# Sink attention and mixer: two heads share each transpose, and value products run on crossed 64x64 quarters

## The chip, the cores and the metric

The kernel runs on one core of one Trainium2 chip. The metric is the device time of one execution in microseconds (us), a median over runs. Five engines work side by side: PE (matrix products; PEld loads its weights), DVE (VectorE), ACT (ScalarE), POOL (GpSimd) and SP, which here only issues DMAs. PE writes to PSUM, which has eight banks; DVE and ACT read PSUM, POOL works on SBUF alone.

## The reference, cut to what matters

```python
# q, k, v: [4, 8, 768, 64]; n_sink = 4, window = 128
scores = scale * np.matmul(q, k.transpose(0, 1, 3, 2))
keep = is_sink | ((rel >= 0) & (rel < window))     # rel = query - key
a = softmax(np.where(keep, scores, -1e9))
x = np.matmul(a, v)                                # heads side by side: [4, 768, 512]
h = x.transpose(0, 2, 1) @ U @ V                   # U: 768 x 32, V: 32 x 768
u = x + h.transpose(0, 2, 1)
out = u + np.maximum(u @ w_ch1, 0.0) @ w_ch2       # 512 -> 2048 -> 512
```

Everything is float32. The two large products of the feed-forward part are made as sums of products of high and low parts, which is most of PE's work.

## The kernel before

**Stages.** Batch 0 comes first and alone: attention, then the rank-32 mixing (`mix_start`, `mix_half`, `mix_end`), about 62 us in which PE has no feed-forward work yet, since that needs batch 0's mixed activations. From there PE runs the feed-forward part of batch 0 (`ffn`, lines 1111 to 1133) and then of batches 1 to 3 (`ffn_joint`, line 1281), and the attention of batches 1 to 3 is laid between these products. DVE, ACT and POOL meanwhile also rebuild the weights from raw 64-bit words (lines 151 to 159: `nr`, `nt`, then a joining sum into `big` or `spare`), split them into high and low parts (line 656 or 657, and line 663 or 665 for the difference) and evict PE's banks.

**One unit of attention** is a pair of heads times one half of the queries; a half takes 64 of each 128 queries, six slices of 64. There are 4 batches x 4 pairs x 2 halves = 32 units. `scores` (line 794) multiplies on 64x64 quarters of the PE array: the two heads are the row halves, two slices the column halves. A slice sees 192 keys; the oldest 64 and the newest 64 of them share 64 columns, since a query row sees a key of just one of the two. A copy under a mask folds them (line 802). Line 807 adds the mask and takes the minimum of a 128x132 block (4 sinks, 64 folded keys, 64 full keys), line 810 is the exponential, lines 817 to 831 normalise, lines 836 to 838 set the sink columns aside.

**Transposes** (line 849): each head's three blocks of 128 queries x 128 keys go through PE into a bank, one bank for each head. The result `oph` holds for each slice the probabilities against its own key block and against the block before it. So the bank is copied whole (128x384, line 656 on ACT or 657 on DVE), the part for the block before is made with a triangular mask (128x320, line 855 on DVE from the bank or line 857 on POOL from the copy), and POOL then masks the copy in place (128x384, line 860). That is three operations a head, six a unit.

**Values** (line 891): for one unit alone (batch 0), twelve products of 128 rows by 64 columns, the two heads on the two column halves. In batches 1 to 3 both halves of a pair are joined (`JOINED`): 22 products on 64x64 quarters, for the folded keys, and 22 on 128x64 halves. Each product of float32 appears as two rows of the trace. One copy a half brings the result into `xT`.

**Order.** `Plan` simulates the engines with a duration for each step, places every step on one of the engines that its `any` allows, and fixes the order of each engine; `MOVES` and `SEED` are a list of pseudo-random changes to the priorities that set the order. Rings of buffers (`NOP` of `oph`, eight banks) limit how far it runs ahead.

Of the kernel before, what the change touches and what calls it, by code (L numbers as in the profile page):

```python
# [9 lines left out]
F32 = mybir.dt.float32  # L10
# [11 lines left out]
P = 128  # L22
# [11 lines left out]
TW = SW + G  # L34
# [25 lines left out]
SEED = 30000000  # L60
# [14 lines left out]
JOINED = True  # L75
# [15 lines left out]
NOP = 4  # L91
# [93 lines left out]
class Masks:  # L185


    def __init__(self, nc, pool, room):
        self.nc, self.work = nc, pool
        self.m = pool.tile([P, 4, SW], F32, name="mask")  # L190
# [4 lines left out]
        nc.gpsimd.iota(raw, [[-G, 2], [-1, G]], base=P, channel_multiplier=1)  # L195
# [4 lines left out]
        nc.gpsimd.memset(self.m[lo, 0, G:P], -NEG)  # L200
        v.tensor_copy(t[lo, 0:2], raw[lo])
        v.tensor_scalar(t[hi, 0:2], raw[hi], -float(G), None, ALU.add)
        v.tensor_scalar(self.now, t[:, 1], float(G), None, ALU.is_ge)
        v.tensor_scalar(self.past, t[:, 1], float(G), None, ALU.is_lt)
        v.scalar_tensor_tensor(t[:, 0], self.now, -float(P), t[:, 0], ALU.mult, ALU.add)
        v.scalar_tensor_tensor(t[lo, 2], self.past[lo], FAR, t[lo, 0], ALU.mult, ALU.add)
# [3 lines left out]
    def fill(self, ns, w):  # L210
        nc, m, t, lo, hi = self.nc, self.m, self.t, self.lo, self.hi
        v, copy = nc.vector, nc.scalar.copy
        ck = self.work.tile([P, 3, NS], F32, name="m_ck")
        v.tensor_scalar(ck[:, 2], self.cix[:, 0], ns, None, ALU.is_lt)
        v.scalar_tensor_tensor(ck[:, 0:2], self.s, w, ck[:, 2].unsqueeze(1).broadcast_to([P, 2, NS]), ALU.is_ge, ALU.mult)
        rows = lambda x: x.rearrange("p a b -> p (a b)")
        for part, at, src in ((slice(0, P), (1, slice(0, P)), rows(t[:, 0:2])), (hi, (0, slice(0, P)), rows(t[hi, 0:2])),
                              (lo, (0, slice(0, G)), t[lo, 2])):
            v.tensor_scalar(m[part, at[0], at[1]], src, w[part], -NEG, ALU.is_ge, ALU.mult)
# [364 lines left out]
class Fast:  # L584
# [191 lines left out]
    def scores(self, half, js, t0, q, kr, row):  # L776
# [4 lines left out]
        def pieces(kb):  # L781

            if kb:
                return (((0, (kb - 1) * SW + NS + half * G, TW),))
# [1019 lines left out]
```

## Time and profile before

| | us |
|---|---|
| median of 3 runs (670.09 to 672.14) | 670.67 |
| the profiled execution | 671.74 |
| its span, first to last instruction | 670.0 |
| PE busy | 648.8 (97%) |
| DVE / ACT / POOL busy | 527.9 / 426.6 / 248.6 |

A busy PE is not a PE at its peak, because consecutive matrix products overlap; so what PE's share says is that there are few gaps. Which of the other engines matters is read stage by stage: a table of windows gives the busy time of each engine in a stretch, the chain of waits says which engine's instructions followed one another up to the end of a stretch, and the groups by line give a duration for each kind of instruction.

### The profile page before, as it was taken

What the parts mean: (1) busy time and instruction counts of PE and PEld (TensorE: products, weight loads), DVE (VectorE), ACT (ScalarE), POOL (GpSimd) and SP (SyncE); (2) the same over time, 40 slices, a digit from 0 to 9 for tenths busy, and PEclk for the clock granted to TensorE, in tenths of its full rate; (3) what the DMA queues carried; (4) which work ended last, traced back from release to release, by engine and by line L of the source; (5) the groups of instructions that cost most, each with busy time, mean ns of one, the idle gap of its engine ahead of it and who ended that gap; (6) DMA issues with size and microseconds to landing.
All of it is one profiled execution on the core that took longest, in us unless ns stands there. A gap on an engine that the chain in (4) does not pass through costs nothing.

```text
span 670.0 us, 15532 instructions
## 1 busy us (share of the span) xinstructions
PE 648.8 (97%) x5302; PEld 599.0 (89%) x5302; DVE 527.9 (79%) x1481; ACT 426.6 (64%) x1186; POOL 248.6 (37%) x320
## 2 busy tenths in 40 slices
PE   7898999999999999999999999999999999999996
PEld 6665888888889889999989899999999999999996
DVE  6999999889999888688887699578537964773483
ACT  6986788998674379875696774455347626534551
POOL 4741533556435244556365644011212401120120
PEclk8999999999999999999999999999999999999999
DMA  8569999999799799997899778979877789878782
GB/s 272 194 215 349 335 385 321 344 291 353 250 327 359 249 310 384 368 302 239 294 299 361 262 220 260 313 212 326 250 242 254 255 299 365 265 236 265 248 270 95
DMA packets 111720, 191.57 MB, mean 286 GB/s; under 512 B 10256, under 2 KB 46608, under 8 KB 111632
## 3 DMA queue, kind: packets, MB, share of 16 engines
q1 hardware_dynamic: 111200, 189.90, 85.0%
q8 instruction: 44, 0.72, 0.4%
q10 hardware_dynamic: 432, 0.59, 0.3%
q14 instruction: 44, 0.36, 0.2%
HBM read 141.17 MB, written 49.28 MB: 284 GB/s over the span
## 4 chain that ended last, share of the span: by engine, by line
PE 78%; DVE 14%; DMA 4%; issue 1%; ACT 1%; POOL 1%; POOLq 0%; SPq 0%; DVEq 0%; ACTq 0%
PE bank L1281 51%; PE bank L1133 7%; PE bank L891 4%; PE bank L794 4%; PE bank L849 2%; PE bank L1111 2%; PE bank L1113 2%; PE bank L1112 2%; DMA w<-ws 2%; DVE nt L157 1%; DVE p L807 1%; DVE spare L158 1%; DVE w L663 1%; DVE nr L154 1%; DVE spare L663 1%
## 5 line engine op out<-in xcount | busy, mean ns | idle before, releaser
L1281 PE MATMUL bank<-w,w 128*128 128x384 f32 x792 | 156.6, 339 | 1.3 <-DMA w<-ws 1.3
L1281 PEld LDWEIGHTS bank<-w,w 128*128 128x128 f32 x792 | 138.3, 188 | 3.9 <-issue 1.8
L810 ACT ACTIVATE p<-p,mn 128x132 f32<-128x132 f32 x192 | 75.6, 397 | 11.8 <-DVE mn L807 11.3
L1281 PE MATMUL bank<-w,spare 128*128 128x384 f32 x348 | 68.0, 338 | 0.0
L1286 DVE TENSOR_TENSOR big<-bank,big 128x384 f32<-128x384 f32 x84 | 45.0, 552 | 24.8 <-PE bank L1281 24.2
L1281 PEld LDWEIGHTS bank<-w,spare 128*128 128x128 f32 x348 | 61.6, 188 | 0.3 <-DVE w L663 0.2
L1133 PE MATMUL bank<-w,hh 128*128 128x512 f32 x192 | 61.3, 400 | 0.0
L807 DVE CUSTOM_DVE_ANT_0 p<-bank,mask 128x132 f32<-128x132 f32 x192 | 47.7, 289 | 0.1
L665 POOL TENSOR_TENSOR w<-uh,w 128x384 fp32r<-128x384 f32 x18 | 19.9, 1106 | 74.2 <-ACT w L656 63.5
L1111 PE MATMUL bank<-ul,w 128*128 128x384 f32 x128 | 44.5, 347 | 0.7 <-POOL ul L665 0.6
L656 ACT CAST w<-ul 128x384 fp32r<-128x384 f32 x57 | 29.1, 513 | 24.7 <-PE bank L1281 21.5
L857 POOL TENSOR_SCALAR_AFFINE_SELECT oph<-oph 128x320 f32<-128x320 f32 x48 | 28.4, 606 | 43.3 <-ACT oph L656 42.8
L1113 PE MATMUL bank<-uh,w 128*128 128x384 f32 x128 | 43.1, 337 | 0.0
L1112 PE MATMUL bank<-uh,w 128*128 128x384 f32 x128 | 43.1, 336 | 0.0
L1281 PE MATMUL bank<-spare,w 128*128 128x384 f32 x210 | 42.1, 339 | 0.0
L665 POOL TENSOR_TENSOR spare<-spare 128x128 f32<-128x128 f32 (+1 forms) x43 | 29.8, 706 | 32.6 <-DMA ws<-spare 11.4
L794 PE MATMUL bank<-kp,qp 64*64 64x196 f32 (+3 forms) x840 | 39.9, 324 | 1.4 <-DMA kp<-in_k_dram 1.4
L1133 PEld LDWEIGHTS bank<-w,hh 128*128 128x128 f32 x192 | 34.8, 188 | 6.4 <-issue 2.0
L663 DVE TENSOR_TENSOR spare<-spare 128x128 f32<-128x128 f32 (+1 forms) x97 | 38.1, 418 | 1.9 <-ACT spare L656 1.3
L1133 PE MATMUL bank<-w,hl 128*128 128x512 f32 x96 | 38.1, 397 | 1.1 <-DVE hl L1122 1.1
L831 POOL TENSOR_TENSOR p<-p,r 128x396 f32<-128x396 f32 x30 | 26.5, 890 | 31.1 <-DVE r L820 26.3
L891 PEld LDWEIGHTS bank<-oph,vp 128*64 128x64 f32 (+1 forms) x1200 | 33.7, 136 | 4.6 <-issue 2.0
(281 smaller groups left out, 1645.8 us busy)
## 6 DMA issues: line engine op xcount, KB each, us to landing
w<-ws SPq DMA_DIRECT2D x132, 256.0 KB, 4.3
w<-wd SPq DMA_DIRECT2D x102, 256.0 KB, 4.2
big<-in_w_dram SPq DMA_DIRECT2D x32, 512.0 KB, 6.3
ws<-spare SPq DMA_DIRECT2D x32, 512.0 KB, 5.6
spare<-ws SPq DMA_DIRECT2D x60, 256.0 KB, 4.1
wd<-w SPq DMA_DIRECT2D x32, 384.0 KB, 6.2
spare<-wd SPq DMA_DIRECT2D x42, 256.0 KB, 3.7
vp<-in_v_dram SPq DMA_DIRECT2D x15, 384.0 KB, 5.1
```

The costliest lines, as they stand in the source:

```text
L663: ways = {"DVE": (dve(n), lambda: nc.vector.tensor_tensor(dst(), a(), b(), op), pool)}
L665: ways["POOL"] = (gps(n), lambda: nc.gpsimd.tensor_tensor(dst(), a(), b(), op), True)
L794: nc.tensor.matmul(st()[a * G:(a + 1) * G, x * TW + to:x * TW + to + wd], qr()[at, q0:q0 + G], kr()[at, k0:k0 + wd], start=True, stop=True ...
L807: add("DVE", dve(SW), lambda st=st, x=x, j=j, part=part, at=at: nc.vector.tensor_tensor_reduce(part(), st()[:, x * TW + half * G:x * TW + ...
L810: add("ACT", act(SW) + 0.22, lambda part=part, at=at: nc.scalar.activation(part(), part(), AF.Exp, bias=at(mn), scale=-1.0, accum_out=at(sm)),
L891: nc.tensor.matmul(pa()[i * D:(i + 1) * D, c:c + (hi - lo) * G], vr()[at, i, kb, :], mv, start=pa not in begun, stop=last, skip_group_chec ...
L1111: nc.tensor.matmul(ph()[:, :CH], wh, ul()[:, c, :], start=n == 0, stop=False)
L1112: nc.tensor.matmul(ph()[:, :CH], wl, uh()[:, c, :], start=False, stop=False)
L1113: nc.tensor.matmul(ph()[:, :CH], wh, uh()[:, c, :], start=False, stop=n == NC - 1)
L1133: nc.tensor.matmul(acc[k](), a()[:, sl], w()[:, :, at, m:m + P].rearrange("p d o j -> p o d j"), start=not begin and i == 0 and j == 0, st ...
L1281: nc.tensor.matmul(bank()[:, :CH], w()[:, at:at + P], u()[:, d, :] if n > 1 else u(), start=first and i == 1, stop=last and i == 3 * n, sk ...
L1286: add("DVE", dve(CH), lambda: nc.vector.tensor_tensor(x(), bank()[:, :CH], t(), ALU.add), r=(bank,) if t is x else (bank, t), w=(x,), prio ...
```

## The change

**Order of the columns.** For the first head of a pair the key tile gives 2 sinks and then 64 keys for each block, for the second head 64 keys and then 2 sinks (`BW` = 66 columns a block; the layout of `k` in memory changes with it). The reduction writes its result interleaved: column 2c of a 132-wide block belongs to one 66-column block, column 2c + 1 to the other, a step of two floats. The two heads of a query block now lie side by side in `p`. So in the 264 columns of both heads every second one, from a suitable start, is a folded key of the first head (64 of them) and then of the second head (64).

**Transposes.** One bank takes both heads' folded keys, another both heads' full keys: still six transposes of 128x128 a unit, read with a step of two floats. Only the folded bank needs masks: DVE writes both of them straight from the bank (128x384 and 128x320, new line 862). The full bank is copied once into a new tile `opf`. POOL's masking steps are gone.

**Values.** First and second head of a unit now lie on partitions 0 to 63 and 64 to 127, so all value products are 64x64. Two units are always joined (two halves of a pair; in batch 0, two pairs of the same half). The first unit's heads go to column halves 0 and 1, the second unit's to 1 and 0, "crossed", so that four products fill four different quarters; the two heads of a unit are different row halves of the array and write to the same bank, on different partitions. 24 products are for folded keys (20 of them 128 columns wide), 20 to 24 for full keys (64 wide). Because the second unit's heads come out swapped, its result is copied in two pieces of 64 partitions.

**Order.** `SEED` and `MOVES` are another list, so the whole order changes in detail.

```diff
-TW = SW + G
+BW = G + 2
+TW = 3 * BW
...
-SEED = 30000000
+SEED = 510000000
...
-JOINED = True
+VALUES = 2.1
...
-NOP = 4
+NOP = 3
+NOF = 2
...
             for x, j in enumerate(js):
-                part = lambda p=p, i=i, j=j: p()[:, i, j]
+                part = lambda p=p, i=i, j=j: p()[:, j, i]
...
-                    part(), st()[:, x * TW + half * G:x * TW + half * G + SW], self.mask[:, 2 * half + min(j, 1)],
+                    part().rearrange("p (c x) -> p x c", x=2), split(st()[:, at0:at0 + SW]),
+                    split(self.mask[:, 2 * half + min(j, 1), 2 * i:2 * i + SW]),
...
-    def transposes(self, i, half, t0, p):
+    def transposes(self, half, t0, p):
...
-                nc.tensor.transpose(tr()[:, u * P:(u + 1) * P], p()[:, i, u, c:c + P], self.ident)
-        add("PE", 0.30, mms, r=parts + [res], w=(tr,), prio=t0)
-        v3 = lambda: tr()[:, :CH].rearrange("p (u j) -> p u j", u=NB)
-        top, prev = lambda: res()[:, :, 1, :], lambda: res()[:, 1:, 0, :]
-        self.copy(CH, top, v3, psum=True, r=(tr,), w=((res, 1),), prio=t0)
-        self.plan.any({
-            "DVE": (dve(CH - G), lambda: nc.vector.tensor_tensor(
-                prev(), v3()[:, 1:], self.tri[:, half].unsqueeze(1).broadcast_to([P, NB - 1, G]), ALU.mult)),
-            "POOL": (0.126 + (CH - G) * 0.914e-3, lambda: nc.gpsimd.affine_select(
...
-        add("POOL", 0.126 + CH * 0.914e-3, lambda: nc.gpsimd.affine_select(
...
+        for at, box in ((NS + 1 - half, res), (NS + half, full)):
+            tr = self.bank()
...
+                    nc.tensor.transpose(tr()[:, u * P:(u + 1) * P], p().rearrange("p u i w -> p u (i w)")[:, u, at:at + 2 * P - 1:2], self.ident)
...
+        for k, n, to in ((0, NB, lambda: res()[:, :, 1, :]), (1, NB - 1, lambda: res()[:, 1:, 0, :])):
+            add("DVE", dve(n * G), lambda k=k, n=n, to=to: nc.vector.tensor_tensor(
+                to(), v3()[:, NB - n:], self.tri[:, k].unsqueeze(1).broadcast_to([P, n, G]), ALU.mult),
+                r=(banks[0],), w=((res, k),), prio=t0)
+        self.copy(CH, full, lambda: banks[1]()[:, :CH].rearrange("p (u j) -> p u j", u=NB), psum=True,
+                  r=(banks[1],), w=(full,), prio=t0)
...
-    def values(self, parts, t0, vr, xT):
+    def values(self, parts, t0):
...
+        for u in range(NB):
+            for part, (half, *_) in enumerate(parts):
+                wide.append((part, 0, 2 * u + half, u, min(2, NB - u)))
+                if u or half:
+                    slim.append((part, 1, 2 * u + half - 1, u, 1))
+        todo = wide + slim
...
+                    at, to = slice(i * D, (i + 1) * D), (i ^ part) * D
...
+                    nc.tensor.matmul(banks[part]()[to:to + D, u * G:(u + n) * G], vr()[at, block, :], mv,
+                                     start=part not in begun, stop=last, skip_group_check=True)
...
+            for to in (slice(0, P),) if part == 0 else (slice(0, D), slice(D, P)):
+                src = to if part == 0 else slice(D - to.start, D - to.start + D)
+                self.copy(CH, lambda to=to, cols=cols, xT=xT: xT()[to, cols], lambda src=src, part=part: banks[part]()[src, :CH],
+                          psum=True, r=(banks[part],), w=((xT, half),), prio=t0)
...
+            parts.append(self.attend(b, pair, half, t0, q, kr, vr, self.x[b][pair]))
+            if len(parts) == 2:
+                self.values(parts, t0)
+                parts = []
```

**Where the order moves.** Line numbers shift by a few between the two kernels: the fold is line 802 before and 807 after, the reduction 807 and 812, the exponential 810 and 816, DVE's joining sum 158 and 159, POOL's 159 and 160.

DVE in the middle of batch 0's attention, before (`oph` are transposed probabilities, `big` and `nr` raw weights and a scratch tile):

```order
L657 COPY oph_520<-bank_181 128x6x64
L657 COPY pair384a<-psink 128x384
L157 SCALAR_TENSOR_TENSOR nt<-big_101,nr 128x192
L151 TENSOR_SCALAR nr<-big_103 128x384
L820 RECIPROCAL r<-r 128x6
L802 COPY_PREDICATED bank_182<-past,bank_182 128x2x64
L802 COPY_PREDICATED bank_185<-past,bank_185 128x2x64
L807 ISA p_568,mn<-bank_182,mask 128x132
L807 ISA mn 128x1
L855 TENSOR_TENSOR oph_520<-bank_181,tri 128x5x64
```

The same place after:

```order
L158 SCALAR_TENSOR_TENSOR nt<-big_101,nr 128x192
L660 COPY pair384a<-psink 128x384
L152 TENSOR_SCALAR nr<-big_103 128x384
L862 TENSOR_TENSOR oph_551<-bank_182,tri 128x6x64
L862 TENSOR_TENSOR oph_551<-bank_182,tri 128x5x64
L826 RECIPROCAL r<-r 128x6
L807 COPY_PREDICATED bank_183<-now,bank_183 128x2x64
L807 COPY_PREDICATED bank_186<-now,bank_186 128x64
```

Every unit now has two masks of DVE next to each other, where before a unit had a copy or a mask on DVE now and then.

DVE at the end of batch 0's attention, before (`big_103`, `big_104` hold the two halves of V, `vst` its split form):

```order
L154 TENSOR_SCALAR nr<-nr 128x512
L157 SCALAR_TENSOR_TENSOR nt<-big_104,nr 128x384
L155 TENSOR_SCALAR nr<-nr 128x512
L663 TENSOR_TENSOR vst_785<-big_103,vst_785 32x384
L158 TENSOR_TENSOR big_104<-nt,big_104 128x384
L855 TENSOR_TENSOR oph_798<-bank_182,tri 128x5x64
L855 TENSOR_TENSOR oph_801<-bank_184,tri 128x5x64
L663 TENSOR_TENSOR vst_785<-big_104,vst_785 32x384
```

and after:

```order
L158 SCALAR_TENSOR_TENSOR nt<-big_104,nr 128x384
L156 TENSOR_SCALAR nr<-nr 128x512
L862 TENSOR_TENSOR oph_848<-bank_183,tri 128x6x64
L862 TENSOR_TENSOR oph_848<-bank_183,tri 128x5x64
L158 SCALAR_TENSOR_TENSOR nt<-big_105,nr 128x512
L666 TENSOR_TENSOR xhl_865<-bank_182,xhl_865 64x384
L1037 TENSOR_SCALAR pst_918<-bank_185 128x128
L666 TENSOR_TENSOR vst_795<-big_104,vst_795 32x384
```

The joining sums of V (`big<-nt,big`) have left DVE.

POOL over the same stretch, before:

```order
L159 TENSOR_TENSOR big_101<-nt,big_101 128x192
L836 COPY psink<-p_568 128x2x3x4
L857 AFFINE_SELECT oph_763<-oph_763 128x5x64
L831 TENSOR_TENSOR p_665<-p_665,r 128x396
L860 AFFINE_SELECT oph_763<-oph_763 128x6x64
L860 AFFINE_SELECT oph_776<-oph_776 128x6x64
L860 AFFINE_SELECT oph_801<-oph_801 128x6x64
L860 AFFINE_SELECT oph_798<-oph_798 128x6x64
L159 TENSOR_TENSOR spare_189<-nt,spare_189 128x512
```

and after:

```order
L160 TENSOR_TENSOR big_103<-nt,big_103 128x384
L837 TENSOR_TENSOR p_616<-p_616,r 128x3x132
L842 COPY psink<-p_616 128x3x8
L837 TENSOR_TENSOR p_680<-p_680,r 128x3x132
L160 TENSOR_TENSOR big_104<-nt,big_104 128x384
L160 TENSOR_TENSOR spare_189<-nt,spare_189 128x512 x2
L668 TENSOR_TENSOR ul_1028<-xT_470,uh_1015 128x384
```

The selects are gone from POOL, and the joining sums of V and of two weight blocks stand there instead.

## Rows read from the trace of the kernel before

**Rows 1.** The page: busy us of each engine (share, instructions).

```profile
PE 648.8 (97%) x5302; PEld 599.0 (89%) x5302; DVE 527.9 (79%) x1481; ACT 426.6 (64%) x1186; POOL 248.6 (37%) x320
```

**Rows 2.** Windows: length, busy us (instructions) of PE, PEld, DVE, ACT, POOL; clock, DMA.

```profile
13.00:30.00 17.00, 15.00 (x214) 11.22 (x214) 14.96 (x86) 15.67 (x72) 11.53 (x22) 0.90 0.77 269
30.00:46.00 16.00, 14.07 (x151) 10.75 (x152) 15.74 (x58) 14.51 (x54) 11.18 (x18) 1.00 0.53 165
46.00:62.00 16.00, 13.27 (x97) 9.84 (x97) 15.34 (x34) 10.64 (x21) 2.01 (x2) 1.00 0.95 317
62.00:203.00 141.00, 138.35 (x1190) 118.45 (x1189) 132.59 (x369) 113.42 (x305) 66.53 (x80) 1.00 0.95 326
203.00:232.00 29.00, 29.00 (x149) 26.46 (x148) 26.22 (x57) 11.42 (x24) 11.63 (x15) 1.00 0.86 298
```

**Rows 3.** Waits of PE from 62 us on: total us, times, longest.

```profile
PE bank L1281 <- DMA w<-ws: 1.6, 2, 1.3
...
PE bank L1281 <- DMA spare<-ws: 0.3, 1, 0.3
```

**Rows 4.** Chain of waits, 0 to 64 us: shares by line; start us, us, piece.

```profile
by line: DVE p L807 13.7%; DVE bank L802 6.8%; DVE nt L157 6.1%; issue 5.7%; DVE xT L1076 5.7%; DMA sc_raw<-in_limits_dram 5.3%; DVE oph L855 4.4%; DVE w L663 3.9%; DVE spare L158 3.6%; DVE nr L154 2.8%; DVE xT L657 2.8%; DVE nr L155 2.7%; 
...
59.65 2.62 DVE xT L1076 x6
```

**Rows 5.** PE timeline (start us, us) and chain (second row of 285 us): value steps.

```profile
46.48 1.43 PE L891 MATMUL bank<-oph,vp 128*64 128x128 f32 x24
47.74 1.38 PE L891 MATMUL bank<-oph,own 128*64 128x128 f32 x24
...
285.39 2.28 PE bank L891 x88
```

**Rows 6.** That joined step by form: count, busy us, mean ns, idle before.

```profile
L891 PE MATMUL bank<-oph,vp 128*64 128x64 f32 x44 | 1.5, 224 | 0.0
L891 PE MATMUL bank<-oph,vp 64*64 64x64 f32 x44 | 0.9, 222 | 0.0
```

**Rows 7.** DVE by line and form, 0 to 62.5 us: count, busy us, mean ns.

```profile
L807 DVE CUSTOM_DVE_ANT_0 p<-bank,mask 128x132 f32<-128x132 f32 x48 | 12.0, 286 | 0.1
L855 DVE TENSOR_TENSOR oph<-bank,tri 128x320 f32<-128x320 f32 x9 | 4.2, 486 | 0.4 <-ACT oph L656 0.3
...
L1076 DVE TENSOR_TENSOR xT<-xT,bank 128x384 f32<-128x384 f32 x7 | 3.3, 547 | 0.0
...
L158 DVE TENSOR_TENSOR big<-nt,big 128x384 uint16<-128x384 uint16 x2 | 2.3, 1130 | 0.0
L158 DVE TENSOR_TENSOR spare<-nt,spare 128x512 uint16<-128x512 uint16 x3 | 2.3, 750 | 0.2
L657 DVE COPY xT<-bank 128x384 f32<-128x384 f32 x4 | 2.1, 534 | 0.0
...
L657 DVE COPY oph<-bank 128x384 f32<-128x384 f32 x3 | 1.6, 547 | 0.0
...
L657 DVE CAST w<-spare 128x512 fp32r<-128x512 f32 x3 | 1.3, 429 | 0.1
```

**Rows 8.** ACT by line and form, 0 to 62.5 us.

```profile
L656 ACT COPY oph<-bank 128x384 f32<-128x384 f32 x13 | 5.9, 467 | 1.0 <-PE bank L849 1.0
...
L153 ACT ACTIVATE spare<-big 128x512 int32<-128x512 uint32 x6 | 4.0, 671 | 0.0
...
L153 ACT ACTIVATE big<-big 128x384 int32<-128x384 uint32 x2 | 1.1, 564 | 0.0
```

**Rows 9.** POOL by line and form, 0 to 62.5 us.

```profile
L860 POOL TENSOR_SCALAR_AFFINE_SELECT oph<-oph 128x384 f32<-128x384 f32 x16 | 9.3, 598 | 0.6 <-ACT oph L656 0.6
...
L857 POOL TENSOR_SCALAR_AFFINE_SELECT oph<-oph 128x320 f32<-128x320 f32 x7 | 4.2, 603 | 6.7 <-ACT oph L656 6.6
...
L159 POOL TENSOR_TENSOR spare<-nt,spare 128x512 int32<-128x512 int32 x1 | 1.3, 1301 | 13.9 <-DVE nt L157 13.9
```

**Rows 10.** PE by line and form, whole span: transposes.

```profile
L849 PE MATMUL bank<-ident,p 128*128 128x128 f32 x192 | 28.4, 281 | 4.1 <-POOL p L831 3.9
```

More of the change, by code (lines that the diff above doesn't have):

```diff
@@ L865, in values @@
[L865 to L882 removed]
+        res, full = self.oph(), self.opf()
@@ L884, in run @@
+        return res, full
+    def values(self, parts, t0):
+        nc, add = self.nc, self.plan.add
+        wide, slim, banks = [], [], [self.bank() for _ in parts]
+        for u in range(NB):
[4 more added lines that the diff above has]
+        todo = wide + slim
         def run():
             begun = set()
-            for k, (_, pa, tops, kb, lo, hi, at) in enumerate(todo):
-                last = all(t[1] is not pa for t in todo[k + 1:])
-                for i, t in enumerate(tops):
-                    mv = t().rearrange("p u s j -> p (u s j)")[at, lo * G:hi * G]
-                    c = kb * G + (lo % 2 == 0) * G
-                    nc.tensor.matmul(pa()[i * D:(i + 1) * D, c:c + (hi - lo) * G], vr()[at, i, kb, :], mv,
-                                     start=pa not in begun, stop=last, skip_group_check=True)
-                begun.add(pa)
@@ new lines, in values @@
+        add("PE", VALUES, run, r=[x for _, tops, vr, _ in parts for x in (vr, *tops)] + [(xT, half) for half, _, _, xT in parts],
+            w=banks, prio=t0, tiled=True)
+        for part, (half, _, _, xT) in enumerate(parts):
+            cols = slice(half * CH, (half + 1) * CH)
+            for to in (slice(0, P),) if part == 0 else (slice(0, D), slice(D, P)):
+                src = to if part == 0 else slice(D - to.start, D - to.start + D)
+                self.copy(CH, lambda to=to, cols=cols, xT=xT: xT()[to, cols], lambda src=src, part=part: banks[part]()[src, :CH],
+                          psum=True, r=(banks[part],), w=((xT, half),), prio=t0)
@@ L914, in attention, with attend @@
+    def attend(self, b, pair, half, t0, q, kr, vr, xT):
+        row = p, _, sm = self.p(), self.mn(), self.sm()
+        for js in TILES:
+            self.scores(half, js, t0, q, kr, row)
+        self.normalise(pair, half, t0, p, sm, self.sinks[b])
+        return half, self.transposes(half, t0, p), vr, xT
     def attention(self, b, stage, start, step):
@@ L921, in attention @@
             self.x[b].append(self.xT())
-            self.attend(b, pair, (0, 1), t0, q, kr, vr, self.x[b][-1])
+            self.values([self.attend(b, pair, half, t0, q, kr, vr, self.x[b][-1]) for half in range(2)], t0)
     def attention_halves(self, b, half):
@@ L1718, in sink_attention_mixer @@
         nc.gpsimd.memset(tri, 1.0)
-        for half in range(2):
-            nc.gpsimd.affine_select(
-                tri[:, half], tri[:, half], [[-1, G]], ALU.is_ge, 0.0, base=-1 - half * G, channel_multiplier=1)
+        for at in (slice(0, G), slice(G, P)):
+            for x, (step, base) in enumerate(((1, 0), (-1, -1))):
+                nc.gpsimd.affine_select(
+                    tri[at, x], tri[at, x], [[step, G]], ALU.is_ge, 0.0, base=base, channel_multiplier=-step)
         make_identity(nc, ident)
```

156 lines of the change are left out of this document (66 added, 90 removed), and 11 rows, old and new, of the table MOVES.

## The prediction

> **What bounds the kernel now.** I read the page first: PE is busy 648.8 of 670.0 us [rows 1], so what is to be had is either work taken off PE or one of its few gaps. The windows say where the gaps are. From 62 us on PE is idle 2.7 us of 141 and then not at all up to 232 us [rows 2], and its six waits from 62 us to the end sum to 5.2 us (the longest and the shortest kind in [rows 3]). The first 62 us are another regime: PE has only batch 0's attention and mixing, with gaps of 2 to 3 us in each window, while DVE is busy 14.96 of 17, 15.74 of 16 and 15.34 of 16 us [rows 2]. The chain of waits over 0 to 64 us is made of DVE lines almost alone [rows 4]. So the program is a head of some 62 us whose length DVE sets, and a body of some 600 us that is PE's own work. A gain must come from DVE's queue in the head or from PE's instructions in the body; work saved on ACT or POOL counts only if it lets one of these two shrink.
>
> **PE's value products (body).** A joined step takes 2.28 us from its first product to the next instruction, twelve times in batches 1 to 3 [rows 5]. The same step by form [rows 6]: 44 rows on quarters, four at a time, so 11 slots: (0.9 - 0.22)/11 = 0.06 us a slot of 64 columns; 44 rows on halves, two at a time, 22 slots: (1.5 - 0.22)/22 = 0.06 us. That is 33 x 0.06 = 1.98 us, and 0.30 us are left for entering the shape, changing it midway, and leaving. For 128 columns the steps of batch 0 give the price: 12 slots from 46.48 to 47.74 us [rows 5], 1.26 us, of which 10 are 128 wide: (1.26 - 0.12)/10 = 0.11 us. After the change a step has 24 products for folded keys, in four quarters 6 x 2 = 12 slots, 10 of them wide and 2 narrow: 1.10 + 0.12 = 1.22 us; 22 for full keys, 12 slots at most: 0.70 us (0.058 each, unrounded). Together 1.92 us, and about half of the 0.30 us, since the shape no longer changes midway: 2.07 us. The gain is 0.21 us a step, x 12 = **-2.5 us**. As column counts go the work is the same, so I bound it by -3.5 (0.30 saved a step) and 0. Batch 0 goes from 8 x 1.26 to 4 x 2.07 us, but this lies in the head, beside DVE, and is counted at nothing; without that cover it would be another -1.8 us.
>
> **Other PE work.** Scores go from 196 to 198 columns, 1%. Four rows run together, so a unit has 6 slots of 0.11 x 196/128 = 0.17 us, and the body has 24 units: 24 x 6 x 0.0017 = **+0.3 us**. Transposes keep their number (192 rows of 281 ns before [rows 10]); they now read with a step of two floats, which no row of PE shows. Nothing extra is the one end; half speed is the other, 0.11 us for each of 144 rows in the body, +15.8 us. I take nothing, the nearest row being ACT's: writing every second word, 384 elements take 564 ns, writing densely, 512 take 671 ns [rows 8], the same cost an element within the fixed part. [...]
>
> **DVE in the head.** Counting each kernel's order up to the last addition of batch 0's mixing into `xT`: eight masks of 128x384 come (0.547 each, priced by line 1076, also a two-operand step from PSUM), +4.38; one mask of 320 goes, -0.49; three copies into `oph`, -1.64; four copies into `xT`, which ACT now makes, -2.14 [rows 7]. So attention itself costs DVE the same, +0.1. What moves off DVE is weight work, taken by a POOL that is rid of 16 selects of 0.598 us and more [rows 9]: two joining sums of V (1.130 each, -2.26), one joining sum of weights (-0.75), two casts of weights to ACT (-0.86) [rows 7]. Smaller moves both ways about cancel and are left out. Sum: -3.8 us. Neighbouring DVE instructions overlap: six of line 1076 advance the chain 2.62 us, 0.44 each instead of 0.547 [rows 4, 7], a factor of 0.8. So DVE's queue is done **3.0 us** sooner, and the head with it. What hides what it hands over: POOL is busy 2.0 of 16 us in the last window and ACT 10.6 [rows 2], and ACT gains five copies fewer but eight more, +3 x 0.467 [rows 8], and two casts. From both sides: 0, if POOL or ACT end up last in the same places, and -4.5, if PE's waits for POOL's normalising (3.9 us in the whole span [rows 10]) go too.
>
> **DVE in the body.** Every later unit now has two masks that only DVE can make, 0.547 + 0.486, where before POOL made all masks of 384 and some of 320 (in the head all 16 and 7 of 16; nine are DVE's [rows 7, 9]). Between batch 0's mixing and batch 1's, DVE's list grows by 5.4 us, x 0.8 = 4.3. In 62 to 203 us DVE has 141 - 132.6 = 8.4 us idle [rows 2], and PE's products of batch 0 go on to 232 us. So I count nothing; if that cover fails, it is 4.3 us.
>
> **Sum.** 671.74 - 2.5 + 0.3 - 3.0 = 666.5 us for the profiled execution. It lay 1.1 us above the median, so the forecast as a median is **665.5 us**.
>
> **Rivals.** (a) *The head does not follow*: DVE is done earlier but waits for ACT, which is busy 15.67 of 17 and 14.51 of 16 us in the two middle windows [rows 2], or for POOL's slower joining sum (1.301 against 0.750 us [rows 7, 9]). Then only PE's part remains: 668.5. For it speaks how full ACT is; against it, that ACT has over 5 us left in the last window. (b) *More follows*: -4.5 in the head, the higher end of the value gain, and one of PE's later waits: 662. (c) *DVE is short in the body*: 665.5 + 4.3 = about 670. (d) *Crossed quarters exclude one another.* The two heads of a unit are different row halves writing to one bank at the same time; before, rows that ran together on different row halves wrote to different banks, so the trace does not show this. If only two quarters run at a time, a step takes 2 x 1.92 + 0.15 = 4.0 us, +1.7 x 12 instead of -2.5: 665.5 + 23 = 688, slower. It decides from 2.5 us a step on, where the head's 3.0 is used up. [...] (e) *The interleaved write slows DVE's reduction* (0.286 us each [rows 7]). The bounds: nothing, as with ACT above, or as in line 158, where writing two bytes at a step of eight bytes takes 1130/384 = 2.9 ns an element and at a step of four 750/512 = 1.5 ns [rows 7]: +1.4 ns x 132 = 0.19 us each. In the head 48 x 0.19 x 0.8 = +7.5 us; in 62 to 203 us another 7.5, of which 4.1 us of idle remain to absorb: 665.5 + 7.5 + 3.4 = 676, slower. It decides from 0.12 us a reduction on. I take nothing, since these are whole words as in ACT's row.
>
> **How the numbers follow.** Forecast 0.50; (a) 0.15; (b) 0.13; (c) 0.06; (d) 0.05; (e), with the half-speed transposes, 0.11. What a measurement of this kernel can tell from no change is about 0.3%, 2 us, so faster is below 668.7: the forecast, (b) and about a third of (a), 0.68. Within 0.3%: the rest of (a) and (c), 0.16. Slower: (d) and (e), 0.16. The predicted time is the likeliest case, 665.5. The range takes in (b) with 1.5 us of its own spread and (a) and (c) with the spread of their bounds, 660.5 to 672.5, and leaves out (d) and (e).
>
> **What the profile after would show.** The joined step near 2.1 us, its rows all 64x64 in the form list; a step of 4 us is (d). The reduction still at 286 ns, else (e). The transposes still at 281 ns a row. The first product of the feed-forward part about 3 us earlier, with the chain still on DVE before it; if it is on ACT or POOL and no earlier, (a). DVE fuller in 62 to 203 us without more waits of PE, else (c). The forecast is wrong if PE gets new waits in the body, since every one of them counts in full there.

## The result and the profile after

The changed kernel takes **663.76 us** (median of 4 runs, 662.16 to 664.7) against 670.38 us for the kernel before in the same comparison: a ratio of 0.9893, 95% interval 0.9865 to 0.9922. The prediction was 665.5 us with a range of 660.5 to 672.5. The profiled execution took 663.0 us, its span is 661.3 us. In a second comparison the same kernel took 665.11 us (0.9912, interval 0.9893 to 0.9931).

The page's busy times, as in [rows 1]:

```profile
PE 643.3 (97%) x5526; PEld 600.1 (91%) x5526; DVE 517.4 (78%) x1472; ACT 435.9 (66%) x1201; POOL 223.3 (34%) x244
```

PE lost 5.5 us of busy time, POOL 25. The windows, with the columns of [rows 2] (length; busy us of PE, PEld, DVE, ACT, POOL; clock, DMA):

```profile
13.00:30.00 17.00, 13.15 (x252) 10.80 (x256) 16.46 (x89) 16.10 (x72) 7.62 (x12) 0.90 0.71 253
30.00:46.00 16.00, 14.88 (x254) 11.40 (x249) 14.13 (x53) 15.23 (x56) 7.07 (x11) 1.00 0.55 186
46.00:62.00 16.00, 15.09 (x153) 11.08 (x153) 14.64 (x29) 13.67 (x28) 4.98 (x5) 1.00 0.95 336
62.00:203.00 141.00, 140.48 (x1227) 122.95 (x1226) 131.22 (x381) 117.61 (x313) 63.35 (x59) 1.00 0.98 339
203.00:232.00 29.00, 29.00 (x168) 25.77 (x167) 24.91 (x60) 11.07 (x25) 7.12 (x10) 1.00 0.89 295
```

In 62 to 203 us PE now idles 0.5 us where it idled 2.7. The waits of PE from the first product of the feed-forward part on are down from 5.2 us [rows 3] to 1.6, the first of them included:

```profile
PE bank L1279 <- DVE w L666: 0.6, 1, 0.6
PE bank L1109 <- POOL ul L668: 0.5, 1, 0.5
PE bank L979 <- DVE pst L666: 0.5, 1, 0.5
```

The head: that first product starts at 60.25 us, where it started at 63.34 before. PE's timeline (start us, us, instruction, idle before it) and the chain of waits over 0 to 61 us, to be held against [rows 4]:

```profile
60.25 0.44 PE L1109 MATMUL bank<-ul,w 128*128 128x384 f32 x1 [0.54 <-POOL ul L668]
```

```profile
by line: DVE p L812 10.6%; DVE oph L862 7.3%; PE bank L798 7.1%; DMA kp<-in_k_dram 6.3%; DVE bank L807 6.0%; DVE nt L158 5.2%; PE bank L857 4.7%; issue 4.6%; PE bank L889 4.3%; DVE w L666 3.4%; ACT p L834 3.3%; POOL ul L668 3.2%; DVE vsh L6
...
56.96 1.29 POOL spare L160
58.25 1.96 POOL ul L668 x2
```

DVE still leads the chain, but PE's scores, transposes and values now hold 7.1, 4.7 and 4.3% of it, where no line of PE was among the twelve largest before. Its last two pieces are POOL's: a joining sum of weights and the low parts of `u`. DVE's groups in the head (0 to 60 us; count, busy us, mean ns) against [rows 7], then POOL's against [rows 9]:

```profile
L812 DVE CUSTOM_DVE_ANT_0 p<-bank,mask 128x132 f32<-128x132 f32 x48 | 12.0, 290 | 0.1
L862 DVE TENSOR_TENSOR oph<-bank,tri 128x384 f32<-128x384 f32 x8 | 4.4, 547 | 1.3 <-PE bank L857 1.3
...
L862 DVE TENSOR_TENSOR oph<-bank,tri 128x320 f32<-128x320 f32 x8 | 3.8, 481 | 0.5 <-PE bank L857 0.5
```

```profile
L160 POOL TENSOR_TENSOR spare<-nt,spare 128x512 int32<-128x512 int32 x2 | 2.6, 1284 | 10.9 <-DVE nt L158 10.2 <-ACT xhl L659 0.7
L160 POOL TENSOR_TENSOR big<-nt,big 128x384 int32<-128x384 int32 x2 | 2.0, 1014 | 2.7 <-ACT big L154 2.2 <-DVE nt L158 0.5
```

The reduction costs what it did, the masks what they were priced at, and the two joining sums of V and one of the weights have gone from DVE to POOL.

A joined value step in the body (start us, us, piece of the chain), and PE's groups over the same 2 us, against [rows 5, 6]:

```profile
94.25 1.95 PE bank L889 x88
```

```profile
L889 PE MATMUL bank<-oph,vp 64*64 64x128 f32 x40 | 1.3, 274 | 0.0
L889 PE MATMUL bank<-opf,vp 64*64 64x64 f32 x44 | 0.9, 218 | 0.0
...
L889 PE MATMUL bank<-oph,vp 64*64 64x64 f32 x8 | 0.3, 217 | 0.0
```

Ten such steps stand whole in the chain, 1.90 to 2.07 us, 1.97 on average. The transposes over the whole span, products and weight loads, against [rows 10]:

```profile
L857 PE MATMUL bank<-ident,p 128*128 128x128 f32 x192 | 29.5, 289 | 5.9 <-POOL p L837 3.3 <-ACT p L834 2.5
L857 PEld LDWEIGHTS bank<-ident,p 128*128 128x128 f32 x192 | 26.8, 204 | 9.4 <-POOL p L837 7.9 <-issue 0.6 <-DVE w L660 0.3
```

That load took 142 ns in the kernel before.

**Where the 8.7 us of span went.** Busy times overlap (the 40 wide products of 274 ns above are 1.3 us of busy time), so I also summed, over all rows of PE, the time from each product's start to the next one's start, less gaps, and put it to the line of the first. Here are the sums for both kernels and for those of the experiments below. "Head" is the start of the first product of the feed-forward part, "body" from there to the end of the last product, "tail" from that end to the end of the span. Values, transposes, scores and gaps are those of the body. The median is of the kernel's own comparison; the rest is of its profiled execution. All are us.

| kernel | median | head | body | values | transposes | scores | gaps | tail |
|---|---|---|---|---|---|---|---|---|
| before | 670.38 | 63.3 | 601.5 | 27.2 | 14.5 | 28.5 | 4.8 | 5.1 |
| changed | 663.76 | 60.3 | 594.3 | 24.4 | 16.1 | 28.8 | 1.2 | 6.8 |
| changed, again | 665.11 | 61.3 | 596.7 | 24.4 | 16.1 | 28.8 | 3.3 | 6.8 |
| adjacent columns | 662.72 | 61.1 | 594.5 | 24.1 | 14.7 | 28.8 | 2.8 | 6.7 |
| adjacent columns, shorter SP code | 660.20 | 60.2 | 593.6 | 24.1 | 14.7 | 28.8 | 1.6 | 5.4 |
| step of four | 665.71 | 60.4 | 598.1 | 24.1 | 16.4 | 28.8 | 3.0 | 6.8 |
| uncrossed | 689.23 | 65.7 | 615.3 | 45.6 | 16.1 | 28.7 | 1.0 | 6.8 |
| DVE's masks twice | 690.99 | 67.0 | 614.3 | 25.8 | 16.6 | 30.9 | 13.8 | 6.8 |
| POOL's selects added | 677.86 | 65.0 | 605.4 | 25.8 | 17.0 | 29.5 | 7.5 | 6.9 |
| before, no list | 668.75 | 63.7 | 597.7 | 27.1 | 14.0 | 28.2 | 2.3 | 5.2 |
| changed, no list | 668.70 | 59.5 | 600.6 | 24.2 | 15.5 | 28.9 | 5.0 | 7.0 |
| changed, no list, no folds | 668.36 | 59.7 | 599.3 | 24.5 | 15.2 | 28.9 | 5.0 | 7.3 |
| changed, list of before | 672.30 | 61.3 | 601.8 | 24.0 | 15.9 | 29.0 | 6.6 | 7.0 |
| before, list of changed | 687.07 | 65.7 | 613.5 | 27.2 | 14.6 | 28.5 | 13.9 | 5.1 |

Before to changed: head -3.1, body -7.2, tail +1.6. In the body values -2.8, transposes +1.6, scores +0.3 make -0.9. Of the remaining 6 us, 3.6 are gaps of PE. Another 2.5 lie in the lines of the feed-forward part, whose number and shape do not change: they are shorter from start to start (497.9 to 495.4), and what shortens them is not shown.

The second trace of the changed kernel, in the same order, has a body only 4.8 us shorter than before. Of the 2.4 us between the two traces' bodies 1.8 are one pause in the middle of a value step, in which PE waited for nothing that the profile shows (total us, times, longest):

```profile
PE bank L889 <- issue: 1.8, 1, 1.8
```

So of the 6 us about 2 change from one execution to the next.

### The profile page after: what moved, and what is told of

Read it like the earlier page. It is cut to its first block, busy times and chain, and to the rows that moved or that the text cites. A ratio compares the mean times of both kernels' runs of the same rounds, so it can differ in the third digit from the quotient of the medians.

```text
span 661.3 us, 15908 instructions
## 1 busy us (share of the span) xinstructions
PE 643.3 (97%) x5526; PEld 600.1 (91%) x5526; DVE 517.4 (78%) x1472; ACT 435.9 (66%) x1201; POOL 223.3 (34%) x244
## 4 chain that ended last, share of the span: by engine, by line
PE 89%; DVE 7%; DMA 1%; ACT 1%; POOL 1%; issue 1%; SPq 0%; DVEq 0%; ACTq 0%; POOLq 0%
PE bank L1279 53%; PE bank L1131 10%; PE bank L798 5%; PE bank L889 4%; PE bank L1109 3%; PE bank L1111 3%; PE bank L1110 3%; PE bank L857 3%; PE bank L996 1%; DVE p L812 1%; PE bank L979 1%; DVE oph L862 1%; PE bank L1019 1%; PE bank L1072 1%; PE bank L1020 1%; DVE w L666 1%
## 5 line engine op out<-in xcount | busy, mean ns | idle before, releaser
L668 POOL TENSOR_TENSOR spare<-spare 128x128 f32<-128x128 f32 (+1 forms) x56 | 46.4, 841 | 61.5 <-DVE spare L666 14.0
L1131 PE MATMUL bank<-w,hh 128*128 128x512 f32 x192 | 61.3, 400 | 0.0
L668 POOL TENSOR_TENSOR w<-uh,w 128x384 fp32r<-128x384 f32 x17 | 17.4, 1022 | 91.3 <-ACT w L659 78.6
L798 PE MATMUL bank<-kp,qp 64*64 64x198 f32 (+3 forms) x840 | 40.8, 326 | 1.3 <-DMA kp<-in_k_dram 1.3
L666 DVE TENSOR_TENSOR w<-ul,w 128x384 fp32r<-128x384 f32 x50 | 30.6, 618 | 10.8 <-ACT w L659 10.5
L1279 PEld LDWEIGHTS bank<-spare,w 128*128 128x128 f32 x210 | 37.0, 188 | 1.4 <-DVE mn L812 0.3
L834 ACT ACTIVATE p<-p,r 128x132 f32<-128x132 f32 x114 | 36.8, 395 | 0.4 <-DVE r L826 0.3
L798 PEld LDWEIGHTS bank<-kp,qp 64*64 64x64 f32 x840 | 28.9, 139 | 8.5 <-issue 5.0
```

The lines of the kernel that those rows point to most:

```text
L666: ways = {"DVE": (dve(n), lambda: nc.vector.tensor_tensor(dst(), a(), b(), op), pool)}
L668: ways["POOL"] = (gps(n), lambda: nc.gpsimd.tensor_tensor(dst(), a(), b(), op), True)
L798: nc.tensor.matmul(st()[a * G:(a + 1) * G, x * TW + to:x * TW + to + wd], qr()[at, q0:q0 + G], kr()[at, k0:k0 + wd], start=True, stop=True ...
L834: nc.scalar.activation(p()[:, u, i], p()[:, u, i], AF.Copy, scale=r()[:, i * NBLK + u:i * NBLK + u + 1])
L1131: nc.tensor.matmul(acc[k](), a()[:, sl], w()[:, :, at, m:m + P].rearrange("p d o j -> p o d j"), start=not begin and i == 0 and j == 0, st ...
L1279: nc.tensor.matmul(bank()[:, :CH], w()[:, at:at + P], u()[:, d, :] if n > 1 else u(), start=first and i == 1, stop=last and i == 3 * n, sk ...
```

## Experiments

**Two layouts of `p`: adjacent columns, and a step of four.** The first keeps the result and the order of all instructions, and makes the two heads' columns neighbours:

```diff
+def halves(p):
+    return p().rearrange("p u i w -> p u (i w)").rearrange("p u (x i c) -> p u x i c", x=2, i=2)
...
-                part = lambda p=p, i=i, j=j: p()[:, j, i]
+                part = lambda p=p, i=i, j=j: halves(p)[:, j, :, i]
...
-                    part().rearrange("p (c x) -> p x c", x=2), split(st()[:, at0:at0 + SW]),
+                    part(), split(st()[:, at0:at0 + SW]),
...
-        for at, box in ((NS + 1 - half, res), (NS + half, full)):
+        for at, box in (((1 - half) * SW + 2, res), (half * SW + 2, full)):
...
-    ... p().rearrange("p u i w -> p u (i w)")[:, u, at:at + 2 * P - 1:2], self.ident)
+    ... p().rearrange("p u i w -> p u (i w)")[:, u, at:at + P], self.ident)
...
```

What else addresses `p` (normalising, the sink columns, the order of the sinks' values) follows the layout and is left out here.

> The changed kernel with another layout of p: in each block of 264 columns first 66 of head one, 66 of head two, then again 66 and 66, instead of every second column. A transpose then reads 128 adjacent columns; the order of every engine is the same. Theory 1 (a step of two floats slows PE's weight load): the changed kernel's transposes load in 206 ns where the kernel before took 141, and from one matmul's start to the next the 144 transposes of the body take 16.1 us instead of 14.5. Then the loads go back to about 141 ns, the body's transposes to 14.5 us, and the time falls by 1.6 us to 662.2; the head's 48 transposes add at most 0.5 more. Rival (the step is free and the slower load has another cause, the tile or the neighbours in the order): loads stay at 206 ns, 663.8 us. In both, the reduction on VectorE stays at 286 to 291 ns, since its writes in runs of 66 or at a step of two cost the same.

The second reads further apart:

```diff
-    ... p().rearrange("p u i w -> p u (i w)")[:, u, at:at + 2 * P - 1:2], self.ident)
+    ... p().rearrange("p u i w -> p (u i w)")[:, at + u * 8:at + u * 8 + 4 * P - 3:4], self.ident)
```

> The changed kernel with the transposes reading every fourth float of p, so that the value products get other numbers; order, counts and shapes are the same. Theory 1 (the load slows with the bytes that it passes over): 128 floats lie over 2048 bytes instead of 1024, the load goes from 206 to about 336 ns (another 2 x 65), the time between transposes grows by some 0.06 us each, 144 of them in the body +9 us, about 672. Rival (the first step away from dense costs something once, as a start, and no more behind it): 206 ns, 664 us.

The changed kernel ran beside them:

> The changed kernel as it is, to have its time on the same chip as the three kernels beside it. By its earlier runs (662.16 to 664.7 us, median 663.76) 663.8 us, 0.989 of the kernel before.

Measured: changed 665.11 us, adjacent 662.72 us (0.9874 of before, interval 0.9853 to 0.9894), step of four 665.71 us (0.9927, 0.9904 to 0.9949). The weight loads of the transposes (count, busy us, mean ns), first of the kernel before, then with adjacent columns, then with a step of four:

```profile
L849 PEld LDWEIGHTS bank<-ident,p 128*128 128x128 f32 x192 | 22.1, 142 | 9.7 <-POOL p L831 6.8 <-issue 0.6 <-ACT p L810 0.5
```

```profile
L861 PE MATMUL bank<-ident,p 128*128 128x128 f32 x192 | 27.9, 280 | 5.0 <-ACT p L838 2.6 <-POOL p L841 2.3
L861 PEld LDWEIGHTS bank<-ident,p 128*128 128x128 f32 x192 | 22.5, 143 | 9.6 <-POOL p L841 7.2 <-issue 0.9 <-ACT p L838 0.2
```

```profile
L857 PE MATMUL bank<-ident,p 128*128 128x128 f32 x192 | 29.8, 291 | 6.6 <-POOL p L837 3.8 <-ACT p L834 2.8
L857 PEld LDWEIGHTS bank<-ident,p 128*128 128x128 f32 x192 | 27.0, 208 | 10.0 <-POOL p L837 8.6 <-issue 0.9
```

So a load of 128 columns takes 143 ns from neighbours, 204 ns at a step of two floats and 208 at a step of four. Leaving dense costs 61 ns once, and doubling the step another 4. Theory 1 held for the first kernel: the body's transposes go from 16.1 to 14.7 us, 1.4 of the 1.6 expected, which is about 10 ns for each of 144. Its median lies 2.4 us below that of the changed kernel beside it; only the 1.4 are traced to the edit. Theory 1 fell for the second kernel (665.7 us where it expected 672). The reduction stayed at 290 to 292 ns in all three.

**Is it the crossing?**

```diff
-                    at, to = slice(i * D, (i + 1) * D), (i ^ part) * D
+                    at, to = slice(i * D, (i + 1) * D), i * D
...
-                src = to if part == 0 else slice(D - to.start, D - to.start + D)
+                src = to
```

> The changed kernel with the second unit's heads on the same two quarters as the first unit's, not crossed, so that two quarters of the array stay empty; order, counts and shapes of all instructions are the same. Theory 1 (the crossing is what lets four products run at a time): a joined step goes from 1.97 to about 3.9 us, the body's 12 steps cost 23 us more and the time is about 687 us. Rival (the gain is in the shape 64x64 alone, or products to the two halves of one bank go one after another anyway): steps stay near 2 us, 664 us.

Measured: 689.23 us (1.0272, interval 1.0243 to 1.0302). A step of the chain, and PE's groups in it:

```profile
99.72 3.78 PE bank L889 x89
```

```profile
L889 PE MATMUL bank<-oph,vp 64*64 64x128 f32 x40 | 2.4, 272 | 0.0
L889 PE MATMUL bank<-opf,vp 64*64 64x64 f32 x44 | 1.4, 218 | 0.0
```

Each product still takes 272 and 218 ns, but the step takes 3.78 us instead of 1.95, so only half as many run at a time. In the changed kernel's step above four rows of PE start within 20 ns of one another (94.339 to 94.359 us, 269 ns each), and the next four 109 ns after them. The body's values go from 24.4 to 45.6 us, the head 4.4 us later. So it is the crossing that lets four products run together, also where two heads write to one bank at the same time.

**What bounds the head.** Two kernels add work to one engine, in places where the order is otherwise kept.

```diff
-            add("DVE", dve(n * G), lambda k=k, n=n, to=to: nc.vector.tensor_tensor(
-                to(), v3()[:, NB - n:], self.tri[:, k].unsqueeze(1).broadcast_to([P, n, G]), ALU.mult),
-                r=(banks[0],), w=((res, k),), prio=t0)
+            def mask(k=k, n=n, to=to):
+                for _ in range(2):
+                    nc.vector.tensor_tensor(
+                        to(), v3()[:, NB - n:], self.tri[:, k].unsqueeze(1).broadcast_to([P, n, G]), ALU.mult)
+            add("DVE", dve(n * G), mask, r=(banks[0],), w=((res, k),), prio=t0)
```

and, in the other, one `tensor_tensor` as before and behind it

```diff
+                if k == 0:
+                    for _ in range(2):
+                        nc.gpsimd.affine_select(to(), to(), [[0, NB], [1, G]], ALU.is_ge, 0.0, base=P, channel_multiplier=-1)
```

> The changed kernel with both masks of every unit written twice on VectorE, the order else the same: 0.547 + 0.482 us more per unit, 8 units in the head and 24 behind it. Theory 1 (VectorE's queue sets the length of the head): the first product of the feed-forward part comes 8 x 1.03 x 0.8 = 6.6 us later, bounds 5 to 8. Rival (ScalarE or GpSimd bound the head after the change): less than 2 us later. Behind the head VectorE gets 24.7 us more, against 9.8 us idle in 62 to 203 us and 32.7 in 232 to 430: by theory 1 new waits of PE there of 0 to 6 us. In all 670 to 677 us; by the rival 664 to 668.

> The changed kernel with two selects of 128x384 per unit on GpSimd, in place on the masked tile behind VectorE's masks (they keep every element), as many as GpSimd had of that size before; the order else the same. 0.6 us each, 16 in the head, 48 behind it. Theory 1 (the head got shorter because GpSimd, rid of the selects, took over joining sums and splits of weights): the first product of the feed-forward part moves back by 2 to 4 us, to about where it stood before, and some of PE's waits on GpSimd's normalising return: 666 to 670 us. Rival (GpSimd has room for the selects as well, it is busy 20 of the 49 us between 13 and 62): less than 1 us, 664 to 665.

Masks twice, 690.99 us, beyond the 670 to 677 expected: the chain up to the feed-forward part, and its first product:

```profile
by line: DVE oph L864 22.6%; DVE p L812 13.4%; DMA kp<-in_k_dram 7.6%; DVE bank L807 7.0%; DVE nt L158 6.9%; issue 3.9%; DVE w L666 3.1%; POOL ul L668 2.9%; DVE vsh L666 2.6%; DVE spare L159 2.2%; DVE nr L155 2.2%; DVE vst L666 2.2%; DVE nr
```

```profile
66.99 0.45 PE L1111 MATMUL bank<-ul,w 128*128 128x384 f32 x1 [0.57 <-POOL ul L668]
```

The head is 6.7 us longer than in the changed kernel's first trace and 5.6 than in its second, whose clock is the nearer one (0.84 in both halves of 10 to 30 us against 0.83 and 0.85; the first trace has 1.00 and 0.83); 6.6 was expected if DVE sets it, with bounds of 5 and 8. The masks' share of the chain goes from 7.3 to 22.6%. But the body is 17.7 us longer than in the second trace, where 0 to 6 was expected: against 24.7 us of extra DVE work that is nearly three quarters, though DVE had over 40 us idle in 62 to 430 us. A small part of it is the clock (below).

Selects added, 677.86 us, beyond the 666 to 670 expected: two waits of PE (total us, times, longest), and the first product:

```profile
PE bank L857 <- POOL p L837: 8.1, 6, 3.0
PE bank L893 <- POOL oph L867: 4.0, 6, 1.2
```

```profile
65.04 0.44 PE L1113 MATMUL bank<-ul,w 128*128 128x384 f32 x1 [0.55 <-POOL ul L668]
```

The head is 3.7 to 4.8 us longer, a little past where it stood before (63.34). The waits for POOL's normalising, 3.9 us in the kernel before and still 3.3 in the changed one, grow to 8.1. So both are needed: DVE's queue sets the head, and POOL must be free of the selects. The edit does two things at once, though: it fills POOL, and it puts the selects between the masks and the value products, which now wait 4.0 us for them; the two are not told apart. Here too the body costs more than expected, 8.7 us. My reading, which no run tests, is that this order has little slack in it when one engine is slowed.

**The computation or the order?** Both kernels without their list of moves, then each with the other's:

```diff
-MOVES = (
-    14, 17, 59, 72, ...
-)
+MOVES = ()
```

> The kernel before with an empty MOVES, so that the plan's own priorities set the order. It and the changed kernel without MOVES tell whether the 6 to 7 us come from what the change computes or from another list. Both theories: slower than with its list, by some 10 to 30 us (no row shows how much the list is worth).

> The changed kernel with an empty MOVES. Theory 1 (the gain is the structure's: value products -2.8 us, transposes +1.6, scores +0.3, and a DVE queue in the head that is 3 us shorter): 3 to 5 us faster than the kernel before without MOVES, with PE's own time between starts for value products, transposes and scores lower by the same 0.95 us together. Rival (the new list made the head shorter and took PE's waits in the body away): within 2 us of it or slower, while the values still take 24.4 us against 27.2.

> The changed kernel with the SEED and MOVES of the kernel before. Theory (a list is fitted to one kernel's order, and for another it is a random shake): no better than without a list, 668.7 us, and up to 6 us worse, 668 to 675. Rival (lists carry over, the new kernel is better with any): 664 to 666.

> The kernel before with the SEED and MOVES of the changed kernel. Theory (a foreign list is a random shake): 668.8 us, its time without a list, to 675. Rival (the new list is good for either, and the change of the computation brings nothing): about 664 us.

Measured: before without list **668.75 us** (0.9977, interval 0.9961 to 0.9993), changed without list **668.70 us** (0.9962, 0.9938 to 0.9986). With the other's list: changed 672.30 (1.0017, 1.0001 to 1.0034), within the 668 to 675 expected, and before 687.07 (1.023, 1.0178 to 1.0282), 12 us past the 675 that its theory allowed. The expectation that any list is worth 10 to 30 us was far off; the list of the kernel before even costs it 2 us, and the new one is worth 3 to 5 us to the changed kernel, so the 6.6 us between the two can be told as the worth of their lists. Without lists the two kernels take the same time, to within some 2 us by the intervals, and theory 1 (3 to 5 us faster) falls. In the table the structure still shows: head -4.2, values -2.9, transposes +1.6, scores +0.7, tail +1.8. What eats it are waits: the body as a whole is 2.9 us longer. PE's longest waits in the body, changed and before, both without lists:

```profile
PE bank L1125 <- ACT w L653: 1.6, 1, 1.6
PE bank L973 <- DVE pst L660: 1.6, 2, 1.2
PE bank L1014 <- DVE xhl L660: 0.8, 1, 0.8
```

```profile
PE bank L974 <- DVE xT L977: 1.0, 1, 1.0
PE bank L842 <- DVE xT L1069: 0.7, 1, 0.7
```

**Is it DVE that is short there?** The changed kernel without list, and without the folds of batches 1 to 3:

```diff
-            add("DVE", dve(n * G), lambda tiles=tiles: nc.vector.copy_predicated(...), w=(st,), prio=t0)
+            add("DVE", dve(n * G), (lambda: None) if self.batch else fold, w=(st,), prio=t0)
```

> The changed kernel without MOVES, and without VectorE's folds (the copies under a mask, four per unit) in batches 1 to 3; those slices are then left unfolded. The order is the same apart from the 96 missing instructions, about 1.03 us of VectorE per unit, 24.8 us in all. Without MOVES the part behind the head takes 600.6 us, 2.9 more than in the kernel before without MOVES, with gaps of PE of 5.0 us against 2.3. Theory (VectorE is short behind the head, since each unit's two masks are now its own): the gaps and the stretched starts go, and the part behind the head falls by 3 to 5 us, to 596 to 598 us; in all 664 to 666. Rival (those waits are one order's accidents on ScalarE, the DMA and GpSimd): it falls by less than 1.5 us; 667 to 669.

Measured: 668.36 us (0.9963, interval 0.9944 to 0.9982) against 668.70. DVE is busy 13.2 us less (its instructions overlap, so 96 folds are worth less than 24.8: in the changed kernel's first trace the 96 sum to 24.7 us, of which 13.0 us overlap no other DVE instruction), the body is 1.4 us shorter, and the same waits stand at the same places with the same lengths:

```profile
PE bank L1127 <- ACT w L653: 1.6, 1, 1.6
PE bank L975 <- DVE pst L660: 1.6, 2, 1.2
PE bank L1016 <- DVE xhl L660: 0.8, 1, 0.8
```

So DVE's load does not make these waits. What is left is the order: what happens to stand ahead of a weight's split or a cast that PE needs next. That is argued and not tried for any single wait.

**The tail.** From DVE's last addition to the end of the span, the kernel before takes 4.5 us, the changed one 6.2. Raw rows of SP at the end (number, start us, ns, kind, what it waits for), first before, then changed:

```
1173 669.05 28 EVENT_SEMAPHORE $S[108]>= $S[101]>=
1174 669.12 27 EVENT_SEMAPHORE $S[109]>= $S[100]>=

1173 658.85 28 EVENT_SEMAPHORE $S[108]>= $S[101]>=
1174 660.32 27 EVENT_SEMAPHORE $S[109]>= $S[100]>=
```

The wait for the last transfer is over by then (row 1167 in both). Without the list row 1174 waits for other semaphores, and the pause stands ahead of it all the same. (Rows are counted from 0; the expectation below names one row less.) The program has a second path for other values of `n_sink` and `window`; it lies ahead of these rows in the code, and the change makes SP's part of it 36 instructions longer. The last kernel shortens it, on top of the adjacent columns:

```diff
-        for half in range(2):
-            nc.sync.dma_start(vt[half * G:(half + 1) * G], self.v[b, h // 2][rows, half::2])
+        for half, eng in enumerate((nc.sync, nc.scalar)):
+            eng.dma_start(vt[half * G:(half + 1) * G], self.v[b, h // 2][rows, half::2])
```

> The kernel with adjacent columns (dense), and one more edit: in the second path of the program, which is taken for other values of n_sink and window and never runs here, the second of the two loads of V is issued by ScalarE instead of SyncE. This makes SyncE's code in that path 32 instructions shorter, about as long as in the kernel before; the path that runs stays as it is, instruction by instruction. In every kernel with the new second path SyncE's row 1173 starts 1.4 to 2.1 us after row 1172, seven to eleven rows from the end and whatever that row waits for; in none with the old one. Theory (the place of SyncE's last rows in its code makes the pause): the pause goes, from the last addition on VectorE to the end of the span it is 4.5 to 4.6 us instead of 6.1 to 6.4, and the time falls by 1.6 us, from 662.7 to 661.1 us. Rival (the pause belongs to what those rows wait for): no change, 662.7 us.

Measured: **660.20 us** (0.9841, interval 0.9828 to 0.9855), the fastest of all. The pause is gone (row 1174 starts 0.06 us after row 1173), and DVE's last addition lies 4.8 us ahead of the end. That is 1.3 of the 2.5 us between the medians; the head is 0.8 us shorter in this execution (see the clock, below) and the gaps in the body are 1.2 us fewer, so only the 1.3 is the edit's.

## Why the prediction was right, and where it was not

The time fell in the forecast's range, 1.7 us below the forecast. In part that is luck: two terms that stood at nothing cost 3.2 us, and one that wasn't in the sum gave back about twice as much.

- **Head, -3.0 us: right to about 1 us.** Measured -3.1 (-2.0 in the second trace, -4.2 without lists); with the lower clock a head of the same order came about 1 us later (below), and each figure rests on one trace a side. Its working holds: DVE is busy 52.4 us up to the first product of the feed-forward part instead of 56.1, and 3.8 had been summed. That DVE sets the head, and that POOL's relief makes room for the sums, was shown by the two kernels with added work. Rival (a) fell.
- **Value products, -2.5 us: right**, 2.8. The step takes 1.97 us in the chain, 2.03 by the starts of the table (24.4 over 12), where 2.07 was worked out. The working has a slip: 12 slots, 10 wide and 2 narrow, are the 1.26 us of its own row, not 1.22, by which the gain would be 2.0. The step gained more because most of the 0.30 us went, and not half. Rival (d) fell: the crossing works, in one bank too, with 1.97 us a step where (d) had 4.0. Its 0.05 was the author's estimate, on which no row of the kernel before bore.
- **Scores, +0.3 us: right**, 0.3 (the product as written gives 0.24).
- **Transposes at nothing: mis-sized.** They cost 1.6 us in the body. The value was taken from a row in which ACT writes at a step, not from one in which PE loads weights, and no row of the kernel before shows PE at a step; the runs showed a load of 204 ns instead of 142. Half speed, +15.8, was much too high. The load's 61 ns more came to about 10 ns a transpose.
- **DVE in the body, and rival (c).** No new waits of PE came with this list, so counting nothing was right here. That the cover is 8 us of idle was not the reason: with twice the masks the body lost 17.7 us, and without the folds it gained 1.4.
- **Rival (e) fell.** The reduction takes 290 ns, as before (286 to 289), interleaved or not.
- **Two terms were missing.** The tail, +1.6 us, goes with the length of SP's code ahead of its last rows: with that code shortened the tail was 1.3 us shorter. The gaps and stretched starts of PE in the body, -6 us in the first trace and -4 in the second, are the largest single term of the result, and stood only in rival (b), as one of PE's later waits. They go with the order: the same changed computation has gaps of 1.2 and 3.3 us with its list, 5.0 without and 6.6 with the other list, and without lists the kernels tie.

So the step that failed is the sum over the body, which took the kernel's waits as given and priced only the instructions. That the head and the values gain 5 to 7 us together shows in the traces with lists and in those without. That the change as such makes the kernel faster is not shown: with equal treatment, no list on either side, the difference is nothing. Of the changed kernel's losses in that tie, the 1.8 us of the tail and most of the 1.6 of the transposes go with the two edits shown above, but a kernel with both and without a list was not run. Whether the old structure has an order as good as the new one's was not tried and stays open, and so does what in the order makes each single wait.

## What to carry to other kernels

Where a change brings a new order with it, run both versions once with the order left to the planner: here that took away the whole difference, while the rows of each instruction still showed what the structure gains and loses. Lay data so that PE loads neighbouring columns (143 ns a load here against 204), even if another engine has to write in two runs for it (DVE's reduction took 290 to 292 ns either way). When the span ends later than the last instruction explains, look at the raw rows of the engine that ends last: 1.3 us here hung on the length of code that never runs.

## What the runs showed of the hardware

**A load's step.** A weight load of 128x128 floats takes 143, 204 and 208 ns for a step of one, two and four floats, as above.

**The clock early in the program.** The changed kernel's two traces differ in the granted clock between 10 and 20 us. First its first trace, then its second (columns as in the windows above):

```profile
10.00:20.00 10.00, 7.04 (x184) 6.04 (x174) 9.62 (x69) 10.00 (x50) 3.27 (x6) 1.00 0.98 338
20.00:30.00 10.00, 7.12 (x105) 5.42 (x102) 9.84 (x46) 9.10 (x39) 5.20 (x8) 0.83 0.51 178
```

```profile
10.00:20.00 10.00, 7.94 (x132) 6.14 (x130) 8.72 (x61) 9.62 (x46) 2.18 (x5) 0.83 0.95 322
20.00:30.00 10.00, 7.11 (x138) 5.55 (x127) 9.57 (x49) 8.60 (x35) 5.27 (x7) 0.85 0.49 175
```

A 0.83 is a mean: in the first trace the clock record has 0.5 from 26.64 to 30.06 us and 1.00 from 9.58 us up to it. At 0.83 between 10 and 20 us PE is busy longer for fewer products, 7.94 us for 132 against 7.04 for 184, and the head ends 1.1 us later (61.34 us). Between 20 and 30 us both are low. The kernels with another layout of `p` keep the order and bear this out: the one with adjacent columns has 0.83 between 10 and 20 us and a head of 61.1, the two others 1.00 and heads of 60.2 and 60.4. The same order can thus end its head at either time, and differences of 1 us in a head need more than one trace. The trace before has the lower clock there too, but not between 20 and 30 us, so neither trace of the changed kernel is quite its like (same columns):

```profile
15.00:20.00 5.00, 5.00 (x82) 3.85 (x82) 3.57 (x24) 4.34 (x21) 3.44 (x8) 0.82 1.03 402
20.00:25.00 5.00, 3.79 (x66) 2.90 (x66) 4.88 (x23) 4.34 (x19) 2.44 (x5) 1.00 0.70 225
```

In two kernels the clock also falls in the body: it is 0.83 between 320 and 330 us with the step of four and with the masks twice. By these 17% of 10 us, an estimate, up to 1.7 us of those two bodies is the clock's.

**Code that never runs.** SP's pause is 1.4 to 2.1 us in all ten traces with the longer second path, always ahead of row 1174, and absent in the four with the shorter one. In the changed kernel's first trace row 1174 starts 1.47 us after row 1173, eight rows behind the jump (row 1166); in the trace before, as far behind the jump, it starts 0.07 us after it. The runs show that the pause goes with the length of that code; what makes it, no trace here shows.
